# Bias groups beside attention steps take the transposes' single PSUM banks instead of the scores' buffers

## The chip, the core and the metric

The kernel runs on one core of one Trainium2 chip. The metric is the time of one execution on the device, in microseconds (us). The kernel before took 1027.63 us in the median of three runs (1027.01 to 1029.39).

The engines are named as the profile names them: PE is TensorE (matmuls; PEld is its queue of weight loads), DVE is VectorE, ACT is ScalarE, POOL is GpSimd, and SP issues most of the DMAs. Each engine works through its own queue in order; semaphores hold an instruction until what it needs is there or a buffer that it overwrites has been read.

## The reference, cut to what matters

Three layers follow each other: attention with a learned bias, a dense layer with a gate, and a routed layer of eight experts. The change concerns the first alone. Its bias depends on the distance between two positions and on the query's position:

```python
B, H, S, D = 4, 8, 576, 64
scores = q @ k^T / sqrt(D)
psi_rel = log1p(|pos_i - pos_j|)
psi_i = log1p(max(pos_i, 1))
x = (psi_rel / psi_i)[..., None]
h = maximum(x @ w1 + b1, 0.0)
bias = h @ w2
attn = softmax(scores + bias.transpose(2, 0, 1))
out = attn @ v
```

The bias (8 heads, 576 x 576) is the same for all four batches. In a row i it depends only on the distance, and there are `max(i, 575 - i) + 1` distances.

## The kernel before, in words

**The bias phase (`BiasPhase`).** The 576 query rows are cut into 36 groups of 16. For group g, `hidden(g)` makes four tiles "hid" of 128 partitions by `far(g)` distances, `far(g) = max(16 g + 15, 575 - 16 g) + 1`: 576 for the first and the last group, 304 in the middle. DVE makes them (L93), and for two groups in three ACT makes the first of the four (L91). `group(g)` multiplies them with a small block of w2 (L103, four matmuls of 32 output partitions side by side, twice four where there are over 512 distances) into a PSUM tile "bps". ACT then copies it out twice, once mirrored (L106) and once straight (L107), into the tile "bo"; I call this pair the eviction of a group. `store` sends "bo" to DRAM from SP (L114), one group late. Attention later loads the bias from there in tiles of 128 query rows (L200).

**Attention (`Attention`).** A unit is a pair of heads of one batch; a step is a unit and one of its five query tiles. The transposes of a unit's k and q (tiles tp..k, tp..q, and tp..t for the tails) go through PSUM to ACT, which rounds them (L223), and DVE subtracts the rounded from the exact value (L248, L250, "low parts"). `scores` runs twelve matmuls (L264) into two PSUM tiles "s", one for each head; `softmax1` on DVE adds the bias and finds the row extremes, a pass for each head (L284, giving p and nm); `softmax2` on ACT takes exp (L297); `p_transposes` transposes the probabilities in three lots of three blocks (L345, tiles "px"; lot 0 is copied out by DVE at L349, lots 1 and 2 by ACT at L351); `pv_step` multiplies with v (L403, L404), and ACT copies the result out (L408).

**The order.** The schedule is written out by hand. `lead` first runs groups 0 to 13 with the loads and transposes of the first units in between (table BEFORE). Then `lead_steps` runs eleven attention steps, each with two of the groups 14 to 35. On PE the order of one step x is: score matmuls of step x; lots 1 and 2 of the probabilities of step x - 2; a bias group; half of the pv matmuls of step x - 3; a second bias group; the other half; now and then a transpose of k or q (table BESIDE); lot 0 of step x - 1. On ACT: exp of the first head of step x - 1; evictions of lots 1 and 2; eviction of the first group; exp of the second head; eviction of the second group; pv eviction; with hid tiles in between. On DVE: the two softmax passes; the hid tiles of two groups, each three groups ahead of its use; the copy of lot 0.

**PSUM.** [...] In the pool "ps1" the tag "s" has two buffers of two banks, "xt" three buffers of one bank, and "pv" one of one bank. A tag's buffers are given out in turn: a tile waits until the last reader of the tile that had its buffer is done. Before the change each bias group takes one buffer of "s", with a score tile or another group ahead of it; "xt" holds the transposes of k, q, the tails and the probabilities, and a small one for the sums (`spread`).

Of the kernel before, what the change touches and what calls it, by code (L numbers as in the profile page):

```python
# [11 lines left out]
F32 = mybir.dt.float32  # L12
# [28 lines left out]
class BiasPhase:  # L41
# [54 lines left out]

    def group(self, g, hs):
        nc, d = self.tc.nc, self.far(g)
        ps = self.psum.tile([128, 2, 512], F32, name=f"bps{g}", tag="s", bufs=2).rearrange("p c x -> p (c x)")
        for a, z in ((0, min(d, 512)), (512, d)):  # L100
            for n in range(4):
                if a < z:
                    nc.tensor.matmul(ps[32 * n : 32 * n + 32, a:z], self.wbd, hs[n][:, a:z], start=True, stop=True)  # L103
        o = self.pool.tile([128, S + 15], F32, name=f"bo{g}", tag="bo", bufs=6)
        b, r = 16 * g + 15, self.rinv[:, g : g + 1]
        nc.scalar.activation(o[:, 0:b], ps[:, b:0:-1], AF.Copy, scale=r)  # L106
        nc.scalar.activation(o[:, b:], ps[:, 0 : S - 16 * g], AF.Copy, scale=r)  # L107
        return o
# [971 lines left out]
class Moe2:  # L1080
# [129 lines left out]
    def scatter(self, o, ids, group, out=None):  # L1210

        tc = self.tc
        out = self.out if out is None else out
        i = tc.nc.gpsimd.indirect_dma_start(
            out, bass.IndirectOffsetOnAxis(ids.bitcast(U32), 0), o, None, bounds_check=out.shape[0] - 1, oob_is_err=False,
        )
        tc.declare_no_dep(i.ins, group=group, reason="other rows")
        tc.add_to_no_dep_group(group, i.ins)
# [286 lines left out]
```

## Time and profile before

| | |
|---|---|
| median of three runs | 1027.63 us (1027.01 to 1029.39) |
| the profiled execution | 1027.49 us |
| its span | 1025.7 us |
| mean granted TensorE clock | 0.99 |
| TensorE busy | 989.1 us, 96% of the span |
| DVE busy | 752.7 us, 73% |
| ACT busy | 667.4 us, 65% |

The span is the time from the first to the last instruction that the profiler recorded; the time of the execution is 1.8 us longer. All times in the rows are counted from the start of the span. Busy time counts what an engine executes; the ends of matmuls are modelled, so that short waits within a row of matmuls can show as longer matmuls. The granted clock is the share of the full TensorE clock that the throttle let through.

### The profile page before, as it was taken

The page shows a single profiled execution, that of the slowest core. Times are in us where ns is not written, and L with a number is a line of the kernel's source. Part 1 is how long each engine was busy: PE and PEld are TensorE (multiplying, and loading weights), DVE is VectorE, ACT ScalarE, POOL GpSimd, SP SyncE. Part 2 cuts the span into 40 slices and gives each one's busy share as a digit, 9 for nine tenths or more (in the row PEclk, how much of TensorE's full clock was granted, in tenths as well). Part 3 has the DMA queues.
Part 4 walks back from the last instruction along what each step waited for, and adds up shares of the span by engine and source line. Part 5 has one row for each costly group of instructions (what it writes and reads, how often), then busy time and mean ns, then how long its engine had stood idle before and what let it go on. Part 6 is the DMA issues. An engine that isn't in the chain of part 4 may idle for free. (4 is left out here: it accounts for less than half of the span.)

```text
span 1025.7 us, 20038 instructions
## 1 busy us (share of the span) xinstructions
PE 989.1 (96%) x7102; PEld 820.3 (80%) x7102; DVE 752.7 (73%) x1762; ACT 667.4 (65%) x1558; POOL 203.0 (20%) x228
## 2 busy tenths in 40 slices
PE   6699999999999999999999999999999999999995
PEld 2355866666666689988989889899899999999994
DVE  7966688888888689888889889888887454434321
ACT  7787888888888788766665656666875334434321
POOL 9300223232323201010110201101121142222111
PEclk9999999999999999999999999999999999999998
DMA  7756567775865423020210200301223244433500
GB/s 209 214 151 192 163 189 189 204 206 144 243 164 148 138 86 118 24 82 1 65 29 1 93 1 1 94 1 42 85 78 110 71 130 135 129 114 118 207 24 27
DMA packets 112069, 113.29 MB, mean 110 GB/s; under 512 B 62091, under 2 KB 78987, under 8 KB 111964
## 3 DMA queue, kind: packets, MB, share of 16 engines
q1 hardware_dynamic: 106540, 99.66, 34.0%
q0 software_dynamic: 4992, 11.89, 3.8%
q8 instruction: 59, 0.97, 0.4%
q10 hardware_dynamic: 432, 0.39, 0.2%
q14 instruction: 46, 0.38, 0.1%
HBM read 81.89 MB, written 30.08 MB: 109 GB/s over the span
## 5 line engine op out<-in xcount | busy, mean ns | idle before, releaser
L737 PE MATMUL h<-xh,w 128*128 128x384 f32 x768 | 216.0, 342 | 2.2 <-DVE t L756 2.2
L781 PE MATMUL y<-w,gh 128*128 128x512 f32 x576 | 179.3, 392 | 0.0
L737 PEld LDWEIGHTS h<-xh,w 128*128 128x128 f32 x768 | 141.1, 189 | 6.8 <-DVE t L756 2.8
L737 PE MATMUL h<-xl,w 128*128 128x384 f32 x384 | 129.5, 337 | 0.0
L781 PEld LDWEIGHTS y<-w,gh 128*128 128x128 f32 x576 | 107.0, 188 | 16.6
L284 DVE CUSTOM_DVE_ANT_0 p<-s,bias 128x576 f32<-128x576 f32 x144 | 103.5, 752 | 22.4 <-PE s L264 18.3
L1175 PE MATMUL eh<-xh,ew 128*128 128x288 f32 x512 | 116.5, 303 | 0.0
L781 PE MATMUL y<-w,gl 128*128 128x512 f32 x288 | 113.4, 394 | 0.0
L583 POOL TENSOR_SCALAR wc<-wc 128x512 f32<-128x512 f32 x32 | 64.5, 2014 | 241.0 <-ACT wc L578 221.0
L1197 PE MATMUL ey<-ehh,ew 128*128 128x288 f32 x512 | 112.1, 295 | 0.0
L297 ACT ACTIVATE p<-p,nm 128x576 f32<-128x576 f32 x144 | 111.3, 774 | 1.0 <-DVE nm L284 0.9
L1185 DVE SCALAR_TENSOR_TENSOR ehl<-eh,ehh 128x288 fp32r<-128x288 f32 x64 | 29.2, 456 | 108.8 <-ACT ehh L1184 108.8
L1184 ACT ACTIVATE ehh<-eh 128x288 fp32r<-128x288 f32 x64 | 26.3, 410 | 123.7 <-PE ey L1197 122.5
L749 ACT ACTIVATE z<-h 128x384 f32<-128x384 f32 x96 | 46.6, 485 | 81.6 <-PE h L737 81.6
L345 PE MATMUL px<-ident,p 128*128 128x128 f32 x576 | 93.5, 285 | 0.9 <-ACT p L297 0.4
L345 PEld LDWEIGHTS px<-ident,p 128*128 128x128 f32 x576 | 62.7, 141 | 29.3 <-issue 11.6
L1175 PEld LDWEIGHTS eh<-xh,ew 128*128 128x128 f32 x512 | 85.6, 188 | 0.3 <-issue 0.2
L1197 PEld LDWEIGHTS ey<-ehh,ew 128*128 128x128 f32 x512 | 85.4, 188 | 0.4 <-issue 0.4
L755 DVE SCALAR_TENSOR_TENSOR w<-z,h 128x384 f32<-128x384 f32 x96 | 52.9, 551 | 33.7 <-ACT t L750 30.8
L1175 PE MATMUL eh<-xl,ew 128*128 128x288 f32 x256 | 75.5, 295 | 0.0
L1197 PE MATMUL ey<-ehl,ew 128*128 128x288 f32 x256 | 75.4, 294 | 0.0
L264 PE MATMUL s<-kt,qt 64*128 64x288 f32 x768 | 70.8, 309 | 4.3 <-ACT bo L107 3.9
(488 smaller groups left out, 2225.7 us busy)
## 6 DMA issues: line engine op xcount, KB each, us to landing
rw<-in_moe_w SPq DMA_DIRECT2D x64, 256.0 KB
bias_d<-bo SPq DMA_DIRECT2D x36, 295.5 KB
w<-in_moe_w_out SPq DMA_DIRECT2D x16, 512.0 KB
w<-in_moe_w_in SPq DMA_DIRECT2D x16, 512.0 KB
bias<-bias_d SPq DMA_DIRECT2D x16, 288.0 KB
w_d<-wc SPq DMA_DIRECT2D x18, 256.0 KB
xf<-xt_d SPq DMA_DIRECT2D x24, 192.0 KB
xr<-r_d SPq DMA_DIRECT2D x48, 96.0 KB
```

The costliest lines, as they stand in the source:

```text
L264: nc.tensor.matmul(ps[w][:, c, 0:288], r32(q[r, a, 128 * i : 128 * i + 128] if i < 4 else self.tails(u)[:, a, :]), r32(k[r, b, kc : kc + 2 ...
L284: nc.vector.tensor_tensor_reduce(st["p"][:, c].rearrange("p (a x) -> p a x", a=2), st["ps", w][:, :, 0:288], bias[:, c].rearrange("p (a x) ...
L297: nc.scalar.activation(p[:, c], p[:, c], AF.Exp, bias=nm[:, w : w + 1], scale=-1.0, accum_out=self.st[u, "sm"][:, x : x + 1])
L345: nc.tensor.transpose(ps[:, 128 * j : 128 * j + 128], p[:, 128 * n : 128 * n + 128], self.ident)
L583: self.tc.nc.gpsimd.tensor_scalar(c, c, self.LO, self.HI, op0=ALU.max, op1=ALU.min)
L737: nc.tensor.matmul(ps[:, 0 : self.N], a, r32(b[:, k, :]), start=k + i == 0, stop=k == 3 and i == 2)
L749: nc.scalar.activation(z, h, AF.Square)
L755: nc.vector.scalar_tensor_tensor(w, z, self.C4, h, op0=ALU.mult, op1=ALU.mult)
L781: nc.tensor.matmul(self.acc[u, t], r32(a[:, c]), r32(w[:, b, :]), start=m + i == 0, stop=m == 15 and i == 2)
L1175: nc.tensor.matmul(ps[:, 0:SLOT], a, r32(b[:, k, 0:SLOT]), start=k + i == 0, stop=k == 3 and i == 2)
L1185: nc.vector.scalar_tensor_tensor(r32(l), ps[:, 0:SLOT], 0.0, h, op0=ALU.max, op1=ALU.subtract)
L1197: nc.tensor.matmul(st["y", d][:, 0:SLOT], a, r32(b), start=f + i == 0, stop=f == 7 and i == 2)
```

## The change

`group` asks for its PSUM tile in another place. Groups from `Attention.LEAD` (14) on that have at most 512 distances, which are groups 14 to 31, take a tile of one bank from the tag "xt"; groups 0 to 13 and 32 to 35 take a buffer of "s" as before. Matmuls and evictions are the same.

```diff
     def group(self, g, hs):
         nc, d = self.tc.nc, self.far(g)
-        ps = self.psum.tile([128, 2, 512], F32, name=f"bps{g}", tag="s", bufs=2).rearrange("p c x -> p (c x)")
+        if g < Attention.LEAD or d > 512:
+            ps = self.psum.tile([128, 2, 512], F32, name=f"bps{g}", tag="s", bufs=2).rearrange("p c x -> p (c x)")
+        else:
+            ps = self.psum.tile([128, 512], F32, name=f"bps{g}", tag="xt", bufs=3)
         for a, z in ((0, min(d, 512)), (512, d)):
```

The order of the instructions on every engine is the same before and after; what differs is the semaphores that PE's instructions wait for. All lines of the code from there on are numbered three higher after the change. The first place is PE's queue at step 1 of the eleven, from the transposes of unit 3's q (tp3q) to lot 0 of the first probabilities (px_0_0). s_0_0 and s_0_1 are the score tiles of the two heads, bps_633 and bps_651 are groups 16 and 17. Before:

```order
L220 MATMUL tp3q<-ident,qn_205 128x128 [waits DMASW6_49,DMASW5_49]
...
L264 MATMUL s_0_0_605<-kt_348,qt_349 128x288 [waits PE_49,Activation_49]
L264 MATMUL s_0_1_606<-kt_348,qt_349 128x288 [waits PE_49,Activation_49]
...
L103 MATMUL bps_633<-hid_0_516,wbd 32x320 [waits DVE_49]
...
L103 MATMUL bps_651<-hid_0_564,wbd 32x304 [waits DVE_49]
...
L345 MATMUL px_0_0_725<-ident,p_0_560 128x128 [waits Activation_49]
```

After:

```order
L223 MATMUL tp3q<-ident,qn_205 128x128 [waits DMASW6_49,DMASW5_49,DVE_49]
...
L267 MATMUL s_0_0_605<-kt_348,qt_349 128x288 [waits DVE_49]
L267 MATMUL s_0_1_606<-kt_348,qt_349 128x288 [waits DVE_49]
...
L106 MATMUL bps_633<-hid_0_516,wbd 32x320 [waits PE_49,Activation_49]
...
L106 MATMUL bps_651<-hid_0_564,wbd 32x304 [waits DVE_49,PE_49,Activation_49]
...
L348 MATMUL px_0_0_725<-ident,p_0_560 128x128 [waits PE_49,Activation_49]
```

Nothing moved; the score matmuls now wait for DVE where they waited for ACT, and the bias groups for ACT where they waited for DVE. The second place is PE's queue at step 4, where the score matmuls of unit 0's second query tile (s_1_0, s_1_1), lots 1 and 2 of the probabilities and groups 22 and 23 (bps_932, bps_955) stand. Before:

```order
L264 MATMUL s_1_0_894<-kt_272,qt_273 128x288 [waits PE_49,Activation_49]
L264 MATMUL s_1_1_895<-kt_272,qt_273 128x288 [waits PE_49,Activation_49]
...
L345 MATMUL px_0_1_914<-ident,p_0_744 128x128 x3
L345 MATMUL px_0_2_919<-ident,p_0_744 128x128 x3
L103 MATMUL bps_932<-hid_0_778,wbd 32x368 [waits DVE_49]
...
L103 MATMUL bps_955<-hid_0_831,wbd 32x384 [waits DVE_49]
```

After:

```order
L267 MATMUL s_1_0_894<-kt_272,qt_273 128x288 [waits DVE_49]
L267 MATMUL s_1_1_895<-kt_272,qt_273 128x288 [waits DVE_49]
...
L348 MATMUL px_0_1_914<-ident,p_0_744 128x128 [waits PE_49,Activation_49]
...
L348 MATMUL px_0_2_919<-ident,p_0_744 128x128 [waits PE_49,Activation_49]
...
L106 MATMUL bps_932<-hid_0_778,wbd 32x368 [waits DVE_49]
...
L106 MATMUL bps_955<-hid_0_831,wbd 32x384 [waits Activation_49]
```

Here, too, nothing moved; lots 1 and 2, which waited for no buffer of their own before, now wait for the evictions of the groups that had their banks in the step before.

## Rows read from the trace of the kernel before

**Rows 1.** The page, part 1: busy time, share of the span, instructions.
```profile
PE 989.1 (96%) x7102; PEld 820.3 (80%) x7102; DVE 752.7 (73%) x1762; ACT 667.4 (65%) x1558; POOL 203.0 (20%) x228
```

**Rows 2.** Busy time by stage: stretch, length, each engine's busy time, PEclk, DMA share, GB/s.
```profile
37.66:58.11 20.45, 16.23 (x140) 8.73 (x132) 15.11 (x53) 15.92 (x40) 0.00 (x0) 0.88 0.49 129
58.11:99.90 41.79, 40.87 (x434) 23.95 (x433) 28.38 (x72) 34.34 (x86) 0.00 (x0) 1.00 0.68 185
99.90:130.00 30.10, 30.10 (x347) 25.19 (x347) 19.16 (x47) 24.62 (x72) 5.79 (x3) 1.00 0.53 159
```

**Rows 3.** Idle time (us, times) by releaser: before L103; before L264, 37 to 100.
```profile
  DVE nm L284: 14.0, 18
...
  ACT bo L107: 7.6, 11
```

**Rows 4.** Timeline of DVE: start, length, instruction, in brackets the idle time before.
```profile
35.67 0.75 DVE L284 CUSTOM_DVE_ANT_0 p<-s,bias 128x576 f32<-128x576 f32 x1
...
40.66 0.69 DVE L250 SCALAR_TENSOR_TENSOR qt<-tp3q,qt 128x512 fp32r<-128x512 f32 x1 [1.54 <-ACT qt L223]
...
45.95 0.29 DVE L248 TENSOR_TENSOR kt<-tp3t,kt 128x128 fp32r<-128x128 f32 x1 [0.48 <-ACT qd L223]
...
52.90 0.76 DVE L284 CUSTOM_DVE_ANT_0 p<-s,bias 128x576 f32<-128x576 f32 x1 [1.87 <-PE s L264]
...
58.75 0.56 DVE L349 COPY pt<-px 128x384 f32<-128x384 f32 x1 [1.89 <-ACT hid L91]
...
59.94 0.76 DVE L284 CUSTOM_DVE_ANT_0 p<-s,bias 128x576 f32<-128x576 f32 x1 [0.63 <-PE s L264]
```

**Rows 5.** Timeline of PE in steps 0 to 4.
```profile
36.48 2.52 PE L103 MATMUL bps<-hid,wbd 128*32 128x352 f32 x16 [3.06 <-DVE nm L284]
...
45.48 1.05 PE L264 MATMUL s<-kt,qt 64*128 64x288 f32 x11 [0.94 <-ACT bo L107]
...
48.04 1.42 PE L103 MATMUL bps<-hid,wbd 128*32 128x304 f32 x16 [0.70 <-DVE nm L284]
...
51.92 1.06 PE L264 MATMUL s<-kt,qt 64*128 64x288 f32 x11 [1.64 <-ACT bo L107]
...
58.59 1.34 PE L264 MATMUL s<-kt,qt 64*128 64x288 f32 x12
```

**Rows 6.** Busy time in two stretches of lower clock.
```profile
36.00:38.00 2.00, 1.52 (x12) 0.55 (x16) 2.00 (x8) 0.00 (x0) 0.00 (x0) 0.50 0.27 98
51.92:58.11 6.19, 6.19 (x53) 3.67 (x53) 3.87 (x11) 3.95 (x10) 0.00 (x0) 0.72 0.28 77
```

**Rows 7.** Timeline of PE: scores and lots 1 and 2, steps 4, 6, 10.
```profile
59.86 0.88 PE L345 MATMUL px<-ident,p 128*128 128x128 f32 x6
...
69.72 0.39 PE L264 MATMUL s<-kt,qt 64*128 64x288 f32 x1
...
71.32 0.87 PE L345 MATMUL px<-ident,p 128*128 128x128 f32 x6
...
94.22 1.06 PE L264 MATMUL s<-kt,qt 64*128 64x288 f32 x12
95.20 0.88 PE L345 MATMUL px<-ident,p 128*128 128x128 f32 x6
```

**Rows 8.** Timeline of ACT: a group's eviction in step 5, lots 1 and 2 in step 6.
```profile
69.37 0.62 ACT L106 ACTIVATE bo<-bps,rinv 128x415 f32<-128x415 f32 x1
69.86 0.42 ACT L107 ACTIVATE bo<-bps,rinv 128x176 f32<-128x176 f32 x1
...
71.97 0.87 ACT L351 ACTIVATE pt<-px 128x384 f32<-128x384 f32 x2 [0.76 <-PE px L345]
```

**Rows 9.** Busy time in step 4 and in step 7.
```profile
58.11:63.69 5.58, 5.56 (x59) 3.33 (x58) 4.31 (x12) 4.81 (x13) 0.00 (x0) 1.00 0.62 152
75.39:81.54 6.15, 5.97 (x59) 3.30 (x57) 4.79 (x13) 5.40 (x15) 0.00 (x0) 1.00 0.94 252
```

**Rows 10.** Timeline of SP: the load of the bias tile of step 4.
```profile
46.20 1.28 SPq L200 DMA_DIRECT2D bias<-bias_d  x3
```

## Prediction, made before the change was run

> **Terms.** Step x (0 to 10) is one of the attention steps beside which bias groups 14 to 35 run, two to a step: a first group and a second group. S(x) are its score matmuls (L264), M(x) the two DVE passes over them (L284), X0, X1, X2 the lots 0, 1 and 2 of transposes that run in a step, the ring is the three banks of tag "xt", and P is the pair of score buffers of tag "s". Times are microseconds (us) from the start of the span. About 2 us, 0.2%, is what a measurement of this kernel can tell from no change.
>
> **What bounds the kernel now.** I read the page first: TensorE is busy for 96% of the span [rows 1]. So only stretches in which TensorE is idle, or at half clock, have anything to give. The table by stage then finds them: in 37.66 to 58.11 TensorE has 16.23 us of work in 20.45 us, at a mean granted clock of 0.88; in 58.11 to 99.90 it has 40.87 in 41.79; and in 99.90 to 130 it is full [rows 2]. The waits name a loop through P: bias matmuls waited 14.0 us, 18 times, for M, since a group's buffer is one that S has just filled, and from 37 us on S waited 7.6 us, 11 times, for the bias evictions L107, since the next S takes the groups' buffers [rows 3]. These are sums over TensorE's two queues (weight loads and matmuls) and overlap, so they are not the gain; the gain must be read from the chain of each stage.
>
> In the front (steps 0 to 3) DVE is the slow engine, and the loop makes it wait: between 35.67 and 59.94 it idles five times, for 1.54, 0.48, 1.87, 1.89 and 0.63, in all 6.41 us, and works in all the rest [rows 4]. TensorE itself stands 3.06 us before group 14, 0.94 within S(2), 0.70 before group 18 and 1.64 within S(3) [rows 5]. In steps 4 to 10 TensorE is the bound, and P shows as a stretched S: from the start of S to the start of X1 it takes 0.98 us in step 10, where nothing holds it, and 1.60 in step 6 [rows 7].
>
> **The change, part by part.** No instruction is added, removed or moved on any engine; groups 14 to 31 (18 of the 22) get another bank, and so other waits. Matmuls, evictions and DMAs keep their sizes: nothing for those.
>
> (1) S no longer waits for a bias eviction, but for M(x-1) alone; a group no longer waits for M. (2) A group waits instead for the eviction of the tile three places back in the ring: the first group for X0 (DVE), the second for X1 (ACT). X1 and X2 of the next step wait for the evictions of the two groups; X0 waits for X2. These waits are new, and no trace shows them; I bound them by replaying the in-order queues of PE, DVE and ACT with the durations of the rows.
>
> *Front.* Ahead of group 14 stands nothing but tiles that ACT and DVE have long read, so groups 14 and 15 run at 33.5 to 35.0, in the 3.06 us in which TensorE stood [rows 5]. Their evictions leave ACT at 36.5, and the transposes of q for unit 3 run when DVE has read the tile of unit 3's k, just ahead of 35.67. S(1) then needs M(0), which ends at 35.67 + 0.67 + 0.68 = 37.0 [rows 4], and is through at 38.1. From there DVE hardly waits. Between the start of M(0) and that of M(4) lie 24.27 us; less the 6.41 of idle time, 17.86 are work [rows 4], which back to back would end at 53.5. TensorE against it, step by step:
> - S(2) needs M(1). It ends 1.54 earlier than now (40.66 + 0.61 + 1.35 = 42.62): S(2) runs from 41.2, where all but its first matmul start at 45.48 now [rows 4, 5].
> - X2 of step 2 needs the bank of unit 3's tails, as now, until DVE has made their low parts. These begin at 45.95 and take 0.7; without 1.54 and 0.48 of idle time they end at 44.6 [rows 4]. So TensorE stands from 42.7 to 44.7, then does X2 0.44 [rows 7], two groups of 0.71 [rows 5] and X0 0.44: S(3) runs from 47.0, now from 51.92 but for its first matmul [rows 5].
> - S(3) to S(4) is the work of step 4, which takes 5.58 now with 0.29 of stretch [rows 9]: 5.3, and I add 0.4 because X2 of step 3 must wait for the second group's eviction of step 2, behind an exp on ACT. S(4) starts at 52.7, now at 58.59 [rows 5].
> - M(4) follows S(4) by 1.1: 53.8 instead of 59.94, so 0.3 of DVE's 6.41 stays.
>
> **Gain at S(4): 5.9.** Bounds: the 3.06 us of the first wait alone below, all 6.41 us above.
>
> *Steps 4 to 10.* The seven stretches from S to X1 exceed 0.98 by 0.29, 0.15, 0.62, 0.54, 0.02, 0.49 and 0, so 2.1 us in all; the first is 58.59 to 59.86, the last 94.22 to 95.20 [rows 5, 7]. S will find P free, since M(x-1) ended while the groups of step x-1 still ran. Do the ring waits take it back? In step 5 the second group's eviction ends near 70.2, and X1 of step 6 begins at 71.32, X2 0.4 later [rows 7, 8]: if S goes 0.6 earlier, X2 still has half a microsecond. ACT could become the bound: in step 7, its fullest, it works 5.40 of 6.15 us [rows 9], while TensorE without the stretch of 0.54 needs 5.6. It does not, by 0.2 us; the room is in the 0.76 us that it now idles a step for X1 [rows 8]. **Gain 2.1.** Bounds: 0 (every bit goes into ring waits) and 2.1. In steps 9 and 10 groups 32 to 35 still take P and wait as now: 0.
>
> [...]
>
> [...]
>
> *Transfers.* SP issues stores as evictions end, so they come earlier with them, and DMA was only 0.49 busy in 37.66 to 58.11 [rows 2]. The load of the next bias tile, for M(4), goes out at 46.20 now, in 1.28 us [rows 10]; even at that time it would have 6 us to land before 53.8, and its stores end sooner: nothing.
>
> *After 99.9.* TensorE is full there, and what it does is shifted as a whole; a later stage would give the gain back only if something else were late.
>
> **Sum:** 5.9 + 2.1 - 1.0 = 7.0 us. The profiled execution took 1027.49 us (span 1025.7), within the 1027.01 to 1029.39 of the three runs and 0.14 under their median: 1027.49 - 7.0 = **1020.5 us**.
>
> **Rivals.**
> *A, the front's first wait alone.* TensorE fills the 3.06 us and then meets DVE and ACT in a new order, with X1 and X2 behind evictions that stand in ACT's queue behind an exp; the rest goes. For it: ACT's share in both stages is near 80% [rows 2]. Against: DVE's idle stretches all end in something that comes after S or an ACT instruction queued behind a bias eviction. 1027.49 - 3.1 = 1024.4. Chance 0.13.
> *B, the clock.* [...] Chance 0.10.
> *C, slower.* The second group's eviction waits on ACT behind the exp of L297, X2 waits for that, X0 behind X2, and S behind X0: the loop through P comes back through the ring, longer by one eviction of a group, two ACT instructions that take some 0.9 us [rows 8]. It decides from the point where ACT needs more per step than TensorE, now 5.40 against 5.6 [rows 9]. [...] Chance 0.06.
> *D, no gain.* All of it comes back as a wait later, behind transfers after 99.9 that don't move: 1027.5. Against: TensorE is full to 130. Chance 0.06. That the change does not do what it says I leave out: the built order shows the new waits.
>
> **Chances and range.** Forecast 0.65, A 0.13, B 0.10, C 0.06, D 0.06. Faster by over 0.2%: forecast, A and B, 0.88; within 0.2%: D, 0.06; slower: C, 0.06. The forecast's own bounds go from no fall of the clock and 6.41 us in the front (1019.0) to 1.7 for the clock and half of the steady gain (1022.2). Reaching to A and B, and 0.3 or 0.4 beyond each end, gives 1018.6 to 1024.7; C, D and some tail stay out.
>
> **What would show it.** Right: S waits for no L107 between groups 14 and 31; group 14 starts near 33.5; M(4) near 54; DVE's idle time up to M(4) falls from 6.41 to under 2; S to X1 is about 1.0 in each of steps 4 to 10; every later stage is as long as before and 7 us earlier. Wrong: X1 or X2 waiting for L107 in several steps (C or A); 0.50 in the clock in more than one stretch after 33 (B); a stage after 99.9 that is longer (D).

## The result and the profile after

The changed kernel took 1017.54 us in the median of four runs (1017.16 to 1018.85), the kernel before 1027.64 (1027.01 to 1029.39): a ratio of 0.9901 with a 95% interval of 0.9884 to 0.9918. That is 10.1 us less, where 7.0 were forecast (the 1.0 that this sum takes off is a charge for a fall of the clock in the front); the range ended at 1018.6, so the time lies 1.1 us below it. The same pair on another chip (run e5 below) gave 1018.21 against 1026.44, a ratio of 0.9919 (0.9904 to 0.9934), 8.2 us. In us the two intervals are 8.4 to 11.9 and 6.8 to 9.9; they overlap.

The profiled execution took 1017.92 us (span 1016.1); TensorE's share rose by a point and its busy time fell by 5 us. Some of that is work that had run at half clock in the front (0.50 at 36 to 38, [rows 6]); some of it is score matmuls that waits had stretched in the later steps (the two tables below):

```profile
PE 983.9 (97%) x7102; PEld 818.4 (81%) x7102; DVE 751.7 (74%) x1762; ACT 666.9 (66%) x1558; POOL 202.3 (20%) x228
```

I cut both traces at the same three events: the first softmax passes of steps 0, 4 and 11, M(0), M(4) and M(11). The busy time by stage of the kernel before (length, then PE, PEld, DVE, ACT, POOL, then clock, DMA share, GB/s), first from M(0) to M(4), which I call the front, then from M(4) to M(11):

```profile
35.67:59.94 24.27, 19.23 (x160) 10.49 (x161) 17.66 (x61) 17.55 (x44) 0.00 (x0) 0.86 0.49 133
59.94:101.50 41.56, 40.64 (x433) 23.82 (x434) 28.39 (x73) 33.81 (x84) 0.00 (x0) 1.00 0.69 187
```

And after, in the order of the view: the front, 30 us from near the end of step 10 on (compare [rows 2]), and the stretch from M(4) to M(11):

```profile
35.25:52.95 17.70, 15.14 (x145) 9.01 (x146) 17.20 (x61) 15.80 (x40) 0.00 (x0) 1.00 0.68 191
...
90.50:120.60 30.10, 30.10 (x349) 25.24 (x347) 19.10 (x47) 24.62 (x71) 5.78 (x3) 1.00 0.56 168
...
52.95:92.14 39.19, 38.87 (x433) 23.04 (x433) 28.40 (x72) 33.93 (x86) 0.00 (x0) 1.00 0.73 198
```

The front is 6.57 us shorter, the steps from 4 on 2.37, and the 30 us after them are as full as they were. In the front DVE now works 17.20 of 17.70 us and the clock is full; in the steps after it TensorE works 38.87 of 39.19.

DVE's timeline, which had five idle stretches [rows 4], has one, of 0.39, ahead of M(4) (shown are the first pass of each M and, at 43.53, the low parts of the tails):

```profile
35.25 0.75 DVE L287 CUSTOM_DVE_ANT_0 p<-s,bias 128x576 f32<-128x576 f32 x1
...
39.21 0.75 DVE L287 CUSTOM_DVE_ANT_0 p<-s,bias 128x576 f32<-128x576 f32 x1
...
43.53 0.44 DVE L253 SCALAR_TENSOR_TENSOR qd<-tp3t,qd 64x64 fp32r<-64x64 f32 x2
...
44.59 0.76 DVE L287 CUSTOM_DVE_ANT_0 p<-s,bias 128x576 f32<-128x576 f32 x1
...
48.33 0.74 DVE L287 CUSTOM_DVE_ANT_0 p<-s,bias 128x576 f32<-128x576 f32 x1
...
52.95 0.76 DVE L287 CUSTOM_DVE_ANT_0 p<-s,bias 128x576 f32<-128x576 f32 x1 [0.39 <-ACT x L411]
```

TensorE's timeline of the front, against [rows 5]:

```profile
32.92 1.51 PE L106 MATMUL bps<-hid,wbd 128*32 128x352 f32 x16
35.39 0.66 PE L223 MATMUL tp3q<-ident,qn 128*128 128x128 f32 x4 [0.96 <-DVE kt L251]
...
40.70 1.05 PE L267 MATMUL s<-kt,qt 64*128 64x288 f32 x11 [0.21 <-DVE nm L287]
...
43.01 0.55 PE L348 MATMUL px<-ident,p 128*128 128x128 f32 x3 [0.77 <-ACT pt L354]
44.03 1.26 PE L106 MATMUL bps<-hid,wbd 128*32 128x304 f32 x16 [0.47 <-DVE qd L253]
...
47.91 0.55 PE L348 MATMUL px<-ident,p 128*128 128x128 f32 x3 [0.29 <-ACT bo L110]
...
51.77 1.06 PE L267 MATMUL s<-kt,qt 64*128 64x288 f32 x12
```

Groups 14 and 15 follow S(0) at once. There are new ring waits, but in step 2 not the one that the replay had. X2 of step 2 stands 0.77 before 43.01, for ACT's eviction of X1:

```profile
42.46 0.49 ACT L354 ACTIVATE pt<-px 128x384 f32<-128x384 f32 x1
```

It does not stand behind the tails, since it begins at 43.01 and DVE makes the last of their low parts from 43.53 on. It is group 18 that waits for these, 0.47 us, until 44.03. So X2 had the bank of the tile just ahead of it and group 18 that of the tails, four tiles back: the buffers of a tag are not always given out in turn, as I had written ahead of the prediction. X2 of step 3 waits 0.29 for a group's eviction, as in the replay. S(4) starts at 51.77.

In steps 4 to 10 [rows 7] S is not stretched any more. Here are X1 and X2 of step 4, whose S(4) starts at 51.77, with the first group behind them, and S, X1 and X2 of steps 6 and 10:

```profile
52.76 0.88 PE L348 MATMUL px<-ident,p 128*128 128x128 f32 x6
53.56 0.83 PE L106 MATMUL bps<-hid,wbd 128*32 128x368 f32 x8
...
62.28 1.06 PE L267 MATMUL s<-kt,qt 64*128 64x288 f32 x12
63.27 0.87 PE L348 MATMUL px<-ident,p 128*128 128x128 f32 x6
...
84.85 1.06 PE L267 MATMUL s<-kt,qt 64*128 64x288 f32 x12
85.84 0.87 PE L348 MATMUL px<-ident,p 128*128 128x128 f32 x6
```

From S to X1 it is 0.99 each time; in step 6 it was 1.60. On ACT [rows 8] the eviction of step 5's second group ends at 62.9, before lots 1 and 2 of step 6 begin at 63.27, and ACT's idle time before it copies them out is gone:

```profile
62.52 0.42 ACT L110 ACTIVATE bo<-bps,rinv 128x176 f32<-128x176 f32 x1
...
63.92 0.87 ACT L354 ACTIVATE pt<-px 128x384 f32<-128x384 f32 x2
```

The waits that started it [rows 3], idle time by releaser before the bias matmuls (L106, 32 to 100 us) and before the score matmuls (L267, 36 to 100):

```profile
  DVE nm L287: 1.1, 4
...
  DVE nm L287: 2.1, 7
```

The first line is of the bias matmuls: they wait 1.1 us for M instead of 14.0, and groups 32 and 34, which still take P, are in that. The second is of the score matmuls: what they wait for most is now M, and no bias eviction stands in the view.

### The profile page after: what moved, and what is told of

Same layout as the page of the kernel before. It is cut to its first block, busy times and chain, and to the rows that moved or that the text cites. A ratio compares the mean times of both kernels' runs of the same rounds, so it can differ in the third digit from the quotient of the medians.

```text
span 1016.1 us, 20036 instructions
## 1 busy us (share of the span) xinstructions
PE 983.9 (97%) x7102; PEld 818.4 (81%) x7102; DVE 751.7 (74%) x1762; ACT 666.9 (66%) x1558; POOL 202.3 (20%) x228
## 5 line engine op out<-in xcount | busy, mean ns | idle before, releaser
L740 PEld LDWEIGHTS h<-xl,w 128*128 128x128 f32 x384 | 72.9, 190 | 2.5
```

The lines of the kernel that those rows point to most:

```text
L740: nc.tensor.matmul(ps[:, 0 : self.N], a, r32(b[:, k, :]), start=k + i == 0, stop=k == 3 and i == 2)
```

## The experiments

My theory after the result: the front is bound by DVE, and the loop through the scores' buffers made DVE wait; in the later steps it stretched S. The rivals: the clock is the front's gain; TensorE's first wait is; the front and the later steps need each other; and, for what comes behind, rival D. Each stretch from M(0) to M(4) and from M(4) to M(11) is read as above.

### One part alone: e1, e2, e3

```diff
-        if g < Attention.LEAD or d > 512:
+        if not 14 <= g < 22:    # e1; e2: 22 <= g < 32; e3: 14 <= g < 16
```

> Only groups 14 to 21 (steps 0 to 3) take the transposes' banks; groups 22 to 35 stay in the scores' buffers. Theory (loop): the gain of steps 0 to 3 is DVE's idle time, so it is there in full without the later groups: 6.4 to 7.2 us, about 1020.8; the second softmax pass pair of step 4 starts near 53, and steps 5 to 9 keep their stretched score matmuls (1.8 us together). Rival (the parts need each other, as a bank freed late in one step delays the next): under 5 us, over 1022.6.

> Only groups 22 to 31 (steps 4 to 8) take the transposes' banks. Theory (loop): steps 0 to 3 stay as before (softmax of step 4 near 59.9, five idle stretches of DVE of 6.4 us), and the stretched score matmuls of steps 5 to 9 go: 1.8 to 2.3 us, about 1025.5. Rival (the ring takes it back: lots 1 and 2 wait where the scores waited): 0 to 0.7 us, 1027.

> Only groups 14 and 15 (step 0) take the transposes' banks. Theory (DVE's idle time is the price): the score matmuls of step 1 come 3 us earlier, but DVE has only its first idle stretch of 1.54 to win there, and the later ones (0.48, 1.87, 1.89, 0.63) stay: 1.5 to 2.2 us, about 1025.8. Rival A of the prediction (TensorE's first wait of 3.06 is what counts): 3.1 us, 1024.5. [...]

Measured, each against 29 runs of before on the same chip (median 1026.90): e1 1020.74 us (ratio 0.9945, 0.9930 to 0.9959), e2 1024.83 (0.9980, 0.9968 to 0.9992), e3 1026.56 (1.0001, 0.9989 to 1.0012). The two stretches of e1:

```profile
36.25:54.73 18.48, 16.98 (x145) 10.15 (x146) 17.30 (x60) 15.04 (x39) 0.00 (x0) 0.82 0.69 200
54.73:96.24 41.51, 40.45 (x433) 23.63 (x433) 28.39 (x72) 34.16 (x86) 0.00 (x0) 1.00 0.69 188
```

of e2:

```profile
35.29:59.33 24.04, 19.13 (x160) 10.32 (x161) 17.55 (x60) 17.54 (x44) 0.00 (x0) 0.86 0.53 148
59.33:98.57 39.24, 38.92 (x433) 23.07 (x434) 28.39 (x72) 33.67 (x84) 0.00 (x0) 1.00 0.72 197
```

and of e3:

```profile
35.70:57.66 21.96, 16.99 (x148) 9.74 (x145) 17.48 (x61) 16.71 (x43) 0.00 (x0) 0.90 0.54 153
57.66:99.22 41.56, 40.62 (x433) 23.80 (x434) 28.39 (x73) 33.81 (x84) 0.00 (x0) 1.00 0.69 187
```

The two parts are independent: each kernel has the short stretch where its groups moved and the long one of before (24.27, 41.56) where not, and the gains of the runs, 6.2 and 2.1, add up to 8.2 before rounding, as much as the whole change gives on the other chip (10.1 on the first). In e1 the clock fell in the front (0.82 in the mean, below the 0.86 of before), and the front, 18.48 us, was still 5.8 us shorter than before. Rival A falls: with groups 14 and 15 alone, M(4) comes 2.3 us earlier, not 3.1. But of these 2.3 the medians show only 0.3, and the interval of the ratio holds 1. My expectation for the run was wrong; where the rest went, the next run shows.

### The clock held up in the kernel before: e4

```diff
+    FILL = {0: 3, 1: 1, 2: 2}
+    def fill(self, x, tab):
+        n = self.FILL.get(x, 0)
+        if n:
+            ps = self.psum.tile([128, 512], F32, name=f"fill{x}", tag="pv", bufs=1)
+            for _ in range(n):
+                self.tc.nc.tensor.matmul(ps, self.ident, tab[:, 0:512], start=True, stop=True)
...
             self.op(u, i, "X2", x)
+            if x == 0:
+                self.fill(0, bias.tab)
...
             self.op(u, i, "X0", x + 1)
+            if x in (1, 2):
+                self.fill(x, bias.tab)
```

> The kernel before, all groups in the scores' buffers, with six added matmuls of 512 columns into the bank of the weighted values, whose result nobody reads: three after the scores of step 0, one ahead of those of step 2, two ahead of those of step 3, each where TensorE stands idle. They keep TensorE busy, so that the clock should not fall at 36 and at 53, while every wait of the loop stays. Theory (loop): what the clock takes is mostly covered by DVE: 1 to 2.5 us gained, about 1025.8, DVE still idle 4 us or more before the softmax of step 4. Rival (the clock is the front's gain): 5 us or more, under 1022.6.

Measured: 1027.04 us, a ratio of 1.0006 (0.9994 to 1.0017): no change, where I had expected 1 to 2.5 us less. The front:

```profile
35.34:57.75 22.41, 19.59 (x168) 10.15 (x167) 17.57 (x60) 17.42 (x44) 0.00 (x0) 1.00 0.55 151
```

The clock is 1.00, where it was 0.86, and M(4) comes 1.86 us earlier; DVE still waits 4.7 us. So with the loop in place a full clock is worth 1.9 of the 6.57 us, and e1 has 5.8 of them at a low clock (0.82). The clock as the cause of the front's gain falls. That the run was no faster has a reason later in its profile. ACT, which also scales the weights for the dense layer (L578 before; three higher after the change, L591 here), stood behind a load of weights that had not landed, and TensorE behind ACT. The weights instruction concerned in the kernel before, and in e4:

```profile
154.19 0.67 ACT L578 ACTIVATE wc<-w 128x512 f32<-128x512 f32 x1 [0.87 <-DMA w<-in_moe_w_in]
```

```profile
154.25 0.66 ACT L591 ACTIVATE wc<-w 128x512 f32<-128x512 f32 x1 [2.35 <-DMA w<-in_moe_w_in]
```

Counted from M(4) it comes 94.25 us later before, 96.50 in e4. In e4 TensorE then stood, too:

```profile
155.24 0.79 PE L377 MATMUL pv<-pt,vt 128*64 128x320 f32 x1 [1.84 <-ACT pt L356]
```

and from 155 to 160 its clock was 0.66 in the mean, where it was 1.00 before. At the weights instruction the 1.86 us of the front were gone already: it stands at 154.25, against 154.19 before. In e3 the same instruction waited 1.18 us, and 0.6 of its 2.3 us were gone. Rival D, which I had given 0.06, has its place here.

### The changed kernel, three ways: e5 to e8

e5 is the changed kernel again. e6 makes the router's constants later, e7 the stores of the first units' sums, e8 puts one transposed tile elsewhere:

```diff
# e6
-                attn.lead(bias, lambda x: router.begin(cpool, bpool, w_gate) if x == 1 else None)
+                attn.lead(bias, lambda x: router.begin(cpool, bpool, w_gate) if x == 6 else None)
# e7: in BESIDE, ("store_r", 0) to ("store_r", 3) taken out of steps 20 to 23, and
+        24: (("store_r", 0),), 25: (("store_r", 1),), 26: (("store_r", 2),), 27: (("store_r", 3),),
# e8
-        ps = self.psum.tile([128, 512], F32, name=f"tp{u}{nm}", tag="xt", bufs=3)
+        ps = self.psum.tile([128, 512], F32, name=f"tp{u}{nm}", **(dict(tag="pv", bufs=1) if (u, nm) == (3, "t") else dict(tag="xt", bufs=3)))
```

> The changed kernel once more, as the mark for the three beside it and to see how often the clock falls in steps 0 to 3. Theory (the prediction's charge of 1.0 us for a fall that stays was wrong as a rule, right in size): the clock of most runs is near 0.995 and the odd run at 0.993 is 1 to 1.7 us slower. Rival (the fall comes in about half the runs, and the first profile was lucky): the runs split evenly. Median 1017 to 1018, 9 to 10 under before.

> The changed kernel, with the router's constants (nine small DVE instructions, 0.66 to 0.73 us, with their GpSimd work and three small DMAs) made at step 6 instead of step 1. Theory (DVE alone bounds steps 0 to 3 now): the softmax of step 4 comes 0.6 to 0.7 us earlier, and the whole run 0.5 to 0.7 us, since DVE idles in step 6 anyway. Rival (TensorE's stops or ACT bound steps 0 to 3 as much): 0 to 0.2 us.

> The changed kernel, with the stores of the softmax sums of the first four units (eight DMA issues of about 0.65 us on SP) four steps later, at steps 24 to 27 instead of 20 to 23. Rival D's spot: near 150 us ACT stands in its queue behind a load of weights that SP issues late, for 0.7 to 2.4 us from kernel to kernel, and TensorE behind ACT. Theory (that wait is the place where part of a gain is given back): the load goes out 2 us earlier, ACT's wait there goes, and the run is 0.2 to 1 us shorter with less spread. Rival (the wait is hidden): no change.

> The changed kernel, with the transposes of unit 3's tails in the bank of the weighted values (free until step 3) instead of the ring. Lot 2 of step 2 then waits for no DVE work on the tails. Theory (the stops of TensorE of 0.77 and 0.47 us in step 2 are covered by DVE): softmax of step 4 at the same time within 0.2 us, the run the same. Rival (TensorE's stops in step 2 count): 0.5 to 1.2 us gained.

Measured on one chip, before at 1026.44: e5 1018.21 us, e6 1018.14, e7 1016.24 (1015.82 to 1018.09; ratio to before 0.9906, 0.9891 to 0.9921), e8 1017.53 (1016.27 to 1019.42). The fronts, in the order e5, e6, e7, e8:

```profile
35.35:53.05 17.70, 15.16 (x145) 9.03 (x146) 17.20 (x60) 15.83 (x40) 0.00 (x0) 1.00 0.68 192
```

```profile
35.35:52.53 17.18, 14.89 (x145) 8.97 (x146) 16.64 (x52) 15.67 (x40) 0.00 (x0) 1.00 0.62 180
```

```profile
35.72:53.43 17.71, 16.14 (x145) 9.23 (x146) 17.21 (x61) 15.29 (x39) 0.00 (x0) 0.90 0.63 183
```

```profile
36.05:53.96 17.91, 15.64 (x145) 9.61 (x146) 17.30 (x60) 15.30 (x39) 0.00 (x0) 0.90 0.60 162
```

DVE bounds the front: e6 takes 0.56 us of work from it there, and the front is 0.52 shorter. e8 takes the tails out of the ring. X2 of step 2 then waits for nothing, but group 18 waits 1.28 for the eviction of the lots, so the stop moves, and the front is no shorter than that of e7, which had as much low clock:

```profile
45.10 1.26 PE L106 MATMUL bps<-hid,wbd 128*32 128x304 f32 x16 [1.28 <-ACT pt L354]
```

e7 and e8 show by chance what I had charged 1.0 us for: in both the clock fell in the front (0.90 in the mean), and the front takes 17.71 and 17.91, against 17.70 at full clock. e1, the same order up to M(4), has 0.82 in the mean and takes 18.48: by the lengths of its matmuls the clock was low from about 36.4 to 42.9, in e7 from about 38.2 to 41.6. DVE shows where such a fall is covered and where not. In e1:

```profile
49.33 0.75 DVE L287 CUSTOM_DVE_ANT_0 p<-s,bias 128x576 f32<-128x576 f32 x1
...
53.70 0.56 DVE L352 COPY pt<-px 128x384 f32<-128x384 f32 x1 [0.60 <-ACT hid L91]
...
54.73 0.76 DVE L287 CUSTOM_DVE_ANT_0 p<-s,bias 128x576 f32<-128x576 f32 x1 [0.47 <-PE s L267]
```

M(3) stands 13.08 us after M(0) in e1, e7 and e8 as in the changed kernel. What is lost is lost between M(3) and M(4), where TensorE comes late with X0 and S(4): in e1 they start 16.81 and 17.29 us after M(0), in the changed kernel 16.04 and 16.52.

e5 was also to show how often the clock falls. I had expected most runs near 0.995; three of its five had 0.992 or 0.993, so the rival, that it falls in about half of them, is nearer. In the nine runs of the changed kernel on both chips, the five with 0.995 or more have a median of 1017.17 us and the four with 0.993 or less 1018.71. So a fall of the clock somewhere in the run goes with some 1.5 us; in which stage it falls, only a profile shows.

What e6 gained in the front did not come through: its median is that of e5, where 0.5 to 0.7 us were expected. The weights instruction in e5, in e6 and in e7:

```profile
144.83 0.68 ACT L581 ACTIVATE wc<-w 128x512 f32<-128x512 f32 x1 [0.82 <-DMA w<-in_moe_w_in]
```

```profile
144.70 0.67 ACT L581 ACTIVATE wc<-w 128x512 f32<-128x512 f32 x1 [1.13 <-DMA w<-in_moe_w_in]
```

```profile
144.27 0.67 ACT L582 ACTIVATE wc<-w 128x512 f32<-128x512 f32 x1
```

Counted from M(4) it comes after 91.78, 92.17 and 90.84 us: e6 loses 0.39 of its 0.52 there, and e7, which waits for no load, gains 0.94 on e5. In e5 SP issued this load at 141.21, behind two stores of the sums at 139.80 and 140.50; in e7 it went out at 138.31. e7 is 2.0 us faster in the median; about 1 of that is this spot, and where the rest comes from is not shown.

### Both moves, the mark again, and a ring of two: e9, e10, e11

e9 has the edits of e6 and e7, e10 is e7 again, e11 has `bufs=2` for the tag "xt" in all four places.

> The changed kernel with both moves: the router's constants at step 6 and the first four units' stores of sums at steps 24 to 27. Theory (the 0.54 us that the late constants gained up to step 4 came back at the wait of ACT behind the load of weights near 150 us): with that wait gone the gain stays, so 0.4 to 0.7 us under the kernel with the late stores alone, about 1015.6, and ACT waits for no load between 120 and 165. Rival (it is lost elsewhere): as the late stores alone.

> The kernel with the late stores alone once more, as the mark on the same chip: 1016 to 1017, 1.5 to 2 us under the changed kernel and about 10.5 under before.

> The changed kernel with two banks in the ring instead of three, everywhere in attention. Rival C of the prediction, made to happen: in steps 4 to 10 a lot then waits for the tile two places back, lot 1 for the second group's eviction and lot 2 for DVE's copy of lot 0, and the loop through the scores' buffers would be back as a loop through the ring. If the ring of three had little room, the stretch from the softmax of step 4 to that of step 11 (39.2 us with three, 41.6 before the change) grows past 41.6. If its room is large, it stays under 40. I expect 40 to 42 there, and a loss after step 11 too, where lots follow each other faster: 5 to 20 us over the whole run.

Measured against before at 1026.68: e9 1016.16 us (1015.30 to 1017.01), e10 1016.50 (1015.82 to 1017.21), both a ratio of 0.9897 (0.9882 to 0.9913 for e9); e11 1045.22 in one run. e9 was to be 0.4 to 0.7 us faster than e10; their medians are 0.34 apart, and they can't be told from each other. In e9's profile the clock fell in the front (0.90 in the mean), which took 17.61 where e6's took 17.18 at 1.00. No load is waited for at the spot in either. Both medians lie 1.7 to 2.1 us under e5's, on the same chip.

The two stretches of e11:

```profile
35.65:55.69 20.04, 16.46 (x157) 9.48 (x154) 17.48 (x61) 17.02 (x43) 0.00 (x0) 0.90 0.63 171
55.69:96.78 41.09, 39.21 (x433) 23.01 (x432) 28.39 (x72) 34.40 (x86) 0.00 (x0) 1.00 0.69 189
```

With two banks steps 4 to 10 take 41.09 us, almost the 41.56 of before. But the wait is not that of rival C, lots that stand behind a group's eviction: in each of steps 4 to 8 the first group stands 0.31 behind the eviction of a lot, as in step 4:

```profile
56.67 0.82 PE L106 MATMUL bps<-hid,wbd 128*32 128x368 f32 x8 [0.31 <-ACT pt L354]
```

The third bank is worth 1.9 us there and, with the clock at 0.90 in this one run, up to 2.3 in the front. The rest of the 27 us is lost after step 11. I had expected 5 to 20 in all; by which wait that rest goes is not shown.

### The late stores without the change: e12

The edit of e7 in the kernel before.

> The kernel before the change, all groups in the scores' buffers, with the stores of the first four units' sums at steps 24 to 27. Theory (the wait of ACT behind a load near 150 us is a cost of its own, with or without the change): steps 0 to 10 as before (softmax of step 4 near 59.9 us, 6.4 us of idle DVE), ACT waits for no load between 130 and 165, and the run is 1 to 2 us shorter than before, as it was with the change. Rival (the spot matters only once steps 0 to 10 are shorter): within 0.5 us of before.

Measured: 1024.95 us against 1026.44, a ratio of 0.9987 (0.9977 to 0.9997). The weights instruction waits for no load and comes 93.26 us after M(4), 0.99 less than before; the front, at a mean clock of 0.88, takes 23.37. The spot near 150 us costs about 1 us in the profiles with or without the change; the medians moved by 1.5 and 2.0.

## Why the prediction was right or wrong

- **What bounds each stage: right.** DVE in the front, TensorE after it; e6 shows the first by taking 0.56 us from DVE, and 38.87 of 39.19 us the second.
- **The replay of the front: right in its path, wrong in one place, 0.5 too small.** S(4) stands 6.4 us earlier against M(0), where 5.9 were forecast (S(4) at 51.77 after M(0) at 35.25; 58.59 after 35.67 before). The wrong place is X2 of step 2, which I had behind the tails. TensorE was through with step 2 sooner than that, and S(3) ran 10.4 us after M(0) instead of 11.3; but M(3) waits for DVE's own work, so this changed nothing in the sum. M(4) was to keep 0.3 of DVE's 6.41 us of idle time and keeps 0.39. But the 17.86 us that I took for DVE's work were 17.3. Step 3's hidden tiles took 2.60 us in that one profile and 2.41 or 2.42 in all the others, with the front's mean clock between 0.82 and 1.00; why is open. And I counted idle time from recorded ends: back to back, an instruction begins up to 0.1 us before the recorded end of the one ahead (after the change the next begins 2.33 us after these tiles, which are 2.42 long).
- **Steps 4 to 10: right, 0.4 too small.** From S(4) to the end of step 10's lot 0 it is 2.5 us less, for 2.1. What I had left out is that the first group of a step no longer waits for M: in steps 4 to 8 it begins 0.1 to 0.2 us sooner behind X1 (0.90 in step 4 before, 59.86 to 60.76; 0.80 after, 52.76 to 53.56).
- **The clock: this is the step that failed, the term that was mis-sized most.** No run shows the 1.0 that the sum takes off for a fall of the clock in the front, nor the 1.7 in the range. In the front of the profiled execution the clock was 1.00, so the term was 0. A fall does come there in some executions (the front's mean is 0.82 in e1, 0.90 in e7, e8 and e9, 1.00 in e5 and e6), but between the transposes ahead of S(1) and S(2), and not on S(3). S(1) takes 2.11 in e1 and 1.80 in e8, where the changed kernel takes 1.05 for eleven of its twelve matmuls; the sixteen bias matmuls behind it take 2.29 in e7 and 2.24 in e9, where it takes 1.26, as does e10; S(3) takes 1.06 to 1.34 in these four, where it takes 1.45. And a fall costs less than I charged: 0.0 in e7, 0.2 in e8, 0.4 in e9 against e6, and 0.8 in e1, where it lasted about twice as long as in e7. In the kernel before, a full clock in the whole front was worth 1.9 (e4). DVE and not TensorE bounds the front, and its own work covers most of a fall (in e1 all but 0.8 of the 3.3 us that (1 - 0.82) x 18.48 makes).
- **Tiles through the ring and the clock.** The same five tiles a step through three banks went with a clock of 1.00 in the front (the profiled execution, e5) and of 0.82 and 0.90 (e1, e7, e8); before, with three tiles a step, it was 0.86. So these runs don't show that the number of tiles decides whether the clock falls.
- **Transfers and the time after 99.9: right in the sum, wrong in principle.** In this pair of profiles all of it came through: the weights instruction at 154.19 stands at 144.75. That it can be otherwise, e3, e4 and e6 show.
- **What remains of the 3.0 us** between 1020.5 and 1017.54: 1.0 clock, 0.5 front, 0.4 steps 4 to 10; 0.4 because M(0), ahead of which nothing changed, stood at 35.25 instead of 35.67; some 0.2 behind; and 0.4 by which the median lies under the profiled execution. The 0.4 of M(0) are luck: e2, e4 and e12, which leave the front's groups where they were before, have it at 35.29 to 35.50. The 0.2 and the last 0.4 are scatter as far as I know.
- **The range.** Without the charge for the clock the forecast would have been 1019.5. The end of the range, 1018.6, had no fall of the clock in it, so the charge alone does not explain that the time lies below. Two bounds did not hold: the front gave 6.57 us, more than all of DVE's 6.41, and steps 4 to 10 gave 2.4 to 2.5, more than 2.1. The rest is M(0) and scatter. On the other chip the gain was 8.2, inside the range.
- **The rivals.** A, B and C did not happen. e1, with all of the front's gain from groups 14 to 21, is against A. Of B, more falls of the clock, there is this much: a fall comes in the front in some executions, at 0 to 0.8 us. C's waits of the lots were short with three banks (0.29 in step 3); e11 shows that a ring of two costs as much as the old loop, by another wait than C's. D is real in part, at ACT's wait behind a load.

## What to carry to other kernels

A scratch tile that shares a buffer with the tiles of the main loop ties two engines together through its evictions (here bias matmuls waited 14.0 us for M and S 7.6 for evictions, [rows 3]); look for a single bank with room in another ring before anything is made faster, and read from the trace, tile by tile, whose eviction each tile of the ring waits for; don't count places (three banks were enough here, with 39.19 us from M(4) to M(11), two were not, with 41.09). Price a wait by the idle time of the engine that bounds the stage, not by that of the engine that waits, and a fall of the clock the same way. An upper bound taken from idle times of one profile is not a bound: the work between them moves by some tenths, too (17.86 us here as reckoned, 17.3 as it came out). Then look for the next place where a queue stands behind a transfer (ACT's here, for 0.82 to 2.35 us): an edit whose gain is right in its own stage can be gone 90 us later, as the 1.86 us of e4 were.

## What the runs showed of the hardware

Single runs of an unchanged program scatter more than I thought: 29 runs of the kernel before on one chip took 1024.58 to 1029.86 us. The granted clock of a run goes with it: the ten runs with 0.992 or more have a median of 1025.3, the twelve with 0.990 or less 1028.0. The three runs that the prediction was made from showed only part of that.

In e4 the 2.35 us for which ACT stood behind one load also held the work behind it in ACT's queue that needed none of that load: the next copy of transposes (L356) began at 154.81, right behind the weights instruction, and TensorE, which waited for it, stood for 1.84. That is what turned a late load into lost time.
